# Fewer early weight pieces in the last chunk of an attention and two-MoE kernel, more in the two before it

## The chip, the cores and the metric

The kernel runs on one core of a Trainium2 chip. The metric is device time in microseconds (us) of one execution; three runs before the change took 767.27, 767.58 and 767.68 us.

## What is computed

Three parts, each feeding the next; the two layers' inner nonlinearities are softplus and silu.

```python
def _attn_ref(x, state):                     # x (4, 8, 512, 64), state (4, 8, 32, 64)
    scores = scale * np.matmul(x, state.transpose(0, 1, 3, 2))
    ...                                      # softmax over the 32 states
    xread = np.matmul(a, state)
    scores2 = scale * np.matmul(state, x.transpose(0, 1, 3, 2))
    ...                                      # softmax over the 512 tokens
    sread = np.matmul(a2, x)
    return np.concatenate([xread, sread], axis=2)

def _moe_ref(x, w_in, w_out):                # 2176 x 512, d_ff 2048
    h = x @ w_in
    g = np.maximum(h, 0.0) + np.log1p(np.exp(-np.abs(h)))
    return g @ w_out

def _moe2_ref(x, w_gate, w_val, w_out):      # d_ff 1536
    g = x @ w_gate
    silu = g * (1.0 / (1.0 + np.exp(-g)))
    val = x @ w_val
    return silu * val @ w_out
```

Weights arrive as 64-bit floats, seen by the kernel as pairs of 32-bit words.

## The kernel before

Every 32-bit matmul operand is split into a high and a low part (line 91: `low` is the subtraction of the high part), and a product is three matmuls (`mm3`, line 86). The first layer has four chunks of 512 hidden columns; in each chunk four batches of four tiles are worked through. One such tile is a step (a unit in the code), so chunk c is steps 16c to 16c+15, 64 in all. In step n TensorE does `p2` of step n (12 matmuls into the four banks py, at line 89 as all `mm3`), then what is hooked under "pe", then `p1` of step n+4 (6 matmuls into a bank ph). ScalarE takes two softplus copies from ph (h and C), GpSimd subtracts them (l), and p2 uses h and l. After the last tile of a batch VectorE adds the four py banks into yacc (`y_add`, line 453). A bank that these additions have not emptied can't be written again. The framework picks the banks of PSUM and the buffers of SBUF; in the built program step 20's first py group takes the bank of step 19's first addition and its second group that of the third, before and after the change. In step 60, before, only the fourth group takes a bank of step 59's additions; after, the third and the fourth do.

Weights are converted in pieces of 128 x 512. A piece is loaded raw (line 123), copied by ScalarE (`size`, line 132), put together by VectorE with one operation over the exponent words (`head`, line 136) and two with two operands (`tail`, lines 143 and 146), then split by ScalarE and GpSimd (`high`, `low`). A piece of the second layer (tag "made") is written back to DRAM for later use (lines 181, 199, 209). Two kinds: a gv piece (gate and value columns) also needs four GpSimd sums (line 193) and a second split, six GpSimd operations in all; a w piece (second output weight) needs one. The second layer has 36 pieces, three for each of 12 column groups: gv_0, gv_1, w. In names, gv5_1 is group 5's second gv piece and w25 is group 5's w piece (the printed names may leave numbers out, so a trace shows t_gv and t_w).

The first layer's loop (line 796) writes the order of ScalarE, VectorE, GpSimd and SP by hand: hooks by step and kind, run in the order load, pe, dve0, additions of dt 0 and 1, act, pool, additions of dt 2 and 3, dve1, act1. `at_weights` (line 721) hooks a piece with number n and lateness: load at n-4, size at n-1, head in dve0 of n, tail in dve1 of n+late, high and low at n+late+1. `EARLY` (lines 763 and 764) lists the steps of the second-layer pieces that are made inside the first layer, in the order gv0_0, gv0_1, w20, gv1_0, and so on. The remaining pieces are made in the second layer's loop, two steps of which take three pieces (line 835). In the last chunk VectorE also splits yacc (B11, B21) and forms the sums T1 to T4 (lines 469 to 475) that the second layer multiplies (px, pz, py). The second layer's weights come back from DRAM with `load_gw` (line 230).

Of the kernel before, what the change touches and what calls it, by code (L numbers as in the profile page):

```python
# [37 lines left out]
def attention_moe_moe2_kernel(  # L38
# [20 lines left out]
    NCK = F1 // CH  # L59
# [591 lines left out]
    with tc.manual_schedule(engines={ENG.PE}):  # L651
        units = [(c, b, ft) for c in range(NCK) for b in range(B) for ft in range(FT)]
        NU = len(units)
        UC = B * FT
# [66 lines left out]
        def at_weights(n, late, store, key, make):  # L721

            def begin():
                store[key] = make(*key)
            at(max(0, n - 4), "load", begin)
            for m, kind, step in (
                (n - 1, "act1", "size"), (n, "dve0", "head"), (n + late, "dve1", "tail"),
                (n + late + 1, "act", "high"), (n + late + 1, "pool", "low"),
            )[:3 if store is win else 5]:
                if m == FIRST - 1 and n == FIRST:  # L730
                    m, kind = FIRST, "load"
                if m >= FIRST:
                    at(m, kind, lambda step=step: getattr(store[key], step)())

        for c in range(NCK):
# [5 lines left out]
            for i, (store, make, key) in enumerate(pieces):  # L741
                n, late = n0 + i // 2 * FT + i % 2, 2 - 2 * (i % 2)
# [17 lines left out]
        ):  # L760
            at(i, kind, fn, 0)

        EARLY = [(c * UC + n, 0) for c in range(NCK - 1) for n in ((2, 6, 10, 14) if c else (11, 14, 15))]
        EARLY += [((NCK - 1) * UC + n, 0 if n % 4 else 2) for n in (0, 1, 2, 4, 5, 6, 8)]
        for j, (n, late) in enumerate(EARLY):
            at_weights(n, late, made, (j,), second_piece)
            at(n + late + 1, "pool", lambda j=j: made[j,].sums())
# [66 lines left out]

        for k, j in enumerate(range(len(EARLY), 3 * NF)):
            n, half = divmod(k, 2)
# [35 lines left out]
        with tc.manual_schedule(engines={ENG.DVE, ENG.SP}):  # L872
            run2(-1, "load0")
            run2(-1, "load1")
            for n in range(NS2):
                run2(n, "load0")
                run2(n, "load1")
                c = {}
# [86 lines left out]
```

## Time and profile before

| | us |
|---|---|
| median of 3 runs | 767.58 |
| profiled execution | 768.64 |
| its span, first to last instruction | 766.9 |
| TensorE busy (PE) | 732.2 |
| VectorE busy (DVE) | 439.3 |
| GpSimd busy (POOL) | 386.2 |
| ScalarE busy (ACT) | 318.9 |

The profile has one line for an instruction or a group of equal ones: start, duration, engine, source line, operation, output and inputs, count. A bracket at the end gives the idle time of that engine just before and what ended it. Starts are us from the span's start. The span is 1.7 us shorter than the execution. The granted clock is the share of TensorE's full speed that it was given. Step 16 begins at 142.15 us, step 32 near 219, step 48 near 296, and the second layer at 369.63.

### The profile page before, as it was taken

To read this page: it belongs to the slowest core of one execution; us is meant where nothing else is said; L and a number is where in the kernel's file an instruction comes from. 1 tells how busy PE (TensorE), PEld (TensorE's weight loads), DVE (VectorE), ACT (ScalarE), POOL (GpSimd) and SP (SyncE) were. 2 spreads that over 40 slices of the span, in tenths; PEclk is the share of its full clock that TensorE was granted. 3 is DMA by queue.
4 is the path that set the end of the run, shared out by engine and by line. 5 is a ranking of instruction groups with operands and counts; after the bars stand their busy time and mean duration, and the time that the engine had idled before them with its cause. 6 is when DMAs were issued, how large, how long until landed. Compare 5 with 4: busy or idle time off the path is not lost.

```text
span 766.9 us, 9998 instructions
## 1 busy us (share of the span) xinstructions
PE 732.2 (95%) x3640; PEld 571.1 (74%) x3640; DVE 439.3 (57%) x605; ACT 318.9 (42%) x584; POOL 386.2 (50%) x352
## 2 busy tenths in 40 slices
PE   2898999999999999997999999999999999999997
PEld 0455767777777777775778878788888888888885
DVE  4975627876577547589657555465453333343343
ACT  2774436544454445445454434343353223223320
POOL 1655626755565366787486665565462223223222
PEclk9589999999999999999999999999999999999999
DMA  9921103363344324557488998876646645436502
GB/s 349 409 80 56 60 24 107 119 214 138 106 119 160 110 97 151 194 218 221 163 298 309 300 359 302 312 278 235 203 146 236 219 156 224 170 116 221 211 2 109
DMA packets 51072, 143.78 MB, mean 187 GB/s; under 512 B 5712, under 2 KB 18000, under 8 KB 51024
## 3 DMA queue, kind: packets, MB, share of 16 engines
q1 hardware_dynamic: 51024, 143.15, 53.4%
q8 instruction: 28, 0.46, 0.2%
q14 instruction: 20, 0.16, 0.1%
HBM read 107.22 MB, written 35.91 MB: 187 GB/s over the span
## 4 chain that ended last, share of the span: by engine, by line
PE 81%; DMA 5%; DVE 5%; POOL 4%; ACT 2%; issue 2%; SPq 0%; ACTq 0%; DVEq 0%; POOLq 0%
PE py L89 22%; PE px L89 16%; PE po L89 16%; PE ph L89 9%; PE pz L89 7%; PE pt L89 3%; PE pm L374 2%; DMA gw<-gv_d 2%; DMA raw_gv<-in_moe_w_val_dram 2%; PE ps L505 2%; POOL l L92 1%; PE ps L89 1%; PE sc L267 1%; DMA xT<-in_xt_dram 1%; PE pa L335 1%
## 5 line engine op out<-in xcount | busy, mean ns | idle before, releaser
L89 PE MATMUL py<-h,wo 128*128 128x512 f32 x512 | 159.7, 393 | 8.7 <-DVE yacc L453 6.8
L92 POOL TENSOR_TENSOR l<-C,h 128x512 fp32r<-128x512 f32 x64 | 91.7, 1435 | 108.2 <-PE py L89 64.3
L89 PE MATMUL po<-w,h 128*128 128x512 f32 x384 | 126.2, 391 | 0.0
L89 PEld LDWEIGHTS py<-h,wo 128*128 128x128 f32 x512 | 96.2, 189 | 31.1 <-DVE yacc L453 7.6
L92 POOL TENSOR_TENSOR l<-cA,h 128x512 fp32r<-128x512 f32 x24 | 33.7, 1402 | 147.0 <-ACT h L574 147.0
L89 PE MATMUL ph<-aT,m 128*128 128x512 f32 x384 | 102.2, 401 | 0.5 <-POOL aT L92 0.5
L89 PE MATMUL py<-l,wo 128*128 128x512 f32 x256 | 100.0, 391 | 0.0
L89 PEld LDWEIGHTS ph<-aT,m 128*128 128x128 f32 x384 | 70.2, 188 | 28.9 <-issue 12.0
L595 DVE TENSOR_TENSOR oacc<-po,oacc 128x512 f32<-128x512 f32 x80 | 55.1, 690 | 60.5 <-PE po L89 60.0
L89 PEld LDWEIGHTS po<-w,h 128*128 128x128 f32 x384 | 72.1, 188 | 14.9
L404 ACT ACTIVATE h<-ph 128x512 fp32r<-128x512 f32 x64 | 38.2, 598 | 99.2 <-PE ph L89 61.6
L89 PE MATMUL po<-w,l 128*128 128x512 f32 x192 | 74.8, 390 | 0.5 <-POOL l L92 0.5
L89 PE MATMUL px<-T_0s,gw 128*128 128x512 f32 x216 | 61.5, 393 | 4.2 <-ACT cA L883 2.5
L89 PE MATMUL px<-T_1s,gw 128*128 128x512 f32 x216 | 60.7, 389 | 0.0
L89 PEld LDWEIGHTS py<-l,wo 128*128 128x128 f32 x256 | 48.3, 189 | 10.3
L89 PEld LDWEIGHTS px<-T_0s,gw 128*128 128x128 f32 x216 | 39.9, 188 | 14.6 <-ACT cA L883 3.6
L891 DVE TENSOR_TENSOR cA<-py,cA 128x512 f32<-128x512 f32 x24 | 16.6, 690 | 57.5 <-PE py L89 50.4
L574 ACT ACTIVATE h<-cA 128x512 fp32r<-128x512 f32 x24 | 15.1, 631 | 76.9 <-DVE cA L910 76.9
L89 PEld LDWEIGHTS px<-T_1s,gw 128*128 128x128 f32 x216 | 40.5, 188 | 8.5
L89 PEld LDWEIGHTS po<-w,l 128*128 128x128 f32 x192 | 36.0, 188 | 8.3 <-POOL l L92 1.0
L902 ACT ACTIVATE cC<-px 128x512 f32<-128x512 f32 x24 | 14.3, 597 | 64.2 <-PE px L89 60.8
L453 DVE TENSOR_TENSOR yacc<-py,yacc 128x512 f32<-128x512 f32 x48 | 31.5, 686 | 16.1 <-PE py L89 15.9
(147 smaller groups left out, 1348.4 us busy)
## 6 DMA issues: line engine op xcount, KB each, us to landing
gw<-gv_d SPq DMA_DIRECT2D x96, 512.0 KB, 6.5
gv_d<-gv SPq DMA_DIRECT2D x24, 512.0 KB, 3.2
gv_d<-split_gv SPq DMA_DIRECT2D x24, 512.0 KB, 3.5
w<-w_d SPq DMA_DIRECT2D x24, 512.0 KB, 9.2
raw_win<-in_moe_w_in_dram SPq DMA_DIRECT2D x16, 512.0 KB, 6.6
raw_wo<-in_moe_w_out_dram SPq DMA_DIRECT2D x16, 512.0 KB, 4.7
raw_gv<-in_moe_w_gate_dram SPq DMA_DIRECT2D x48, 128.0 KB, 4.4
raw_gv<-in_moe_w_val_dram SPq DMA_DIRECT2D x48, 128.0 KB, 4.1
```

Of the source, the lines that this page charges most:

```text
L89: nc.tensor.matmul(o, a[s], b[t], start=first and i == 0, stop=last and i == 2, **k)
L92: eng.tensor_tensor(out=o, in0=whole, in1=high.bitcast(F32), op=ALU.subtract)
L267: nc.tensor.matmul(self.sc[k * NS:(k + 1) * NS, :], st[q, k, b, :], xT[b, k // 2][q, k % 2, :], start=True, stop=True,)
L335: nc.tensor.transpose(self.ps[:, r * P:(r + 1) * P], self.e[:, r * P:(r + 1) * P], ident)
L374: nc.tensor.matmul(ps[k * NS:(k + 1) * NS, :], st[q, k, b, :], win[c, k].t[q, :], start=True, stop=True)
L404: nc.scalar.activation(self.h, self.ps, AF.Softplus)
L453: nc.vector.tensor_tensor(out=v, in0=yps[dt], in1=v, op=ALU.add)
L505: nc.tensor.matmul(ps, sw[:, kt, :], win[c, kt].t, start=kt == 0, stop=kt == KT - 1)
L574: nc.scalar.activation(h, src, AF.Copy)
L595: nc.vector.tensor_tensor(out=v, in0=ps, in1=v, op=ALU.add)
L891: nc.vector.tensor_tensor(out=c["A"], in0=y, in1=c["A"], op=ALU.add)
L902: nc.scalar.activation(c["C"], x, AF.Copy)
```

## The change

The list of steps at which the early pieces stand. Chunk 0 keeps three pieces; chunks 1 and 2 have six each where they had four (steps 2, 3, 6, 7, 10 and 14 of the chunk); the last chunk has three where it had seven (its steps 0, 1 and 2). The total of 18 stays.

```diff
-        EARLY = [(c * UC + n, 0) for c in range(NCK - 1) for n in ((2, 6, 10, 14) if c else (11, 14, 15))]
-        EARLY += [((NCK - 1) * UC + n, 0 if n % 4 else 2) for n in (0, 1, 2, 4, 5, 6, 8)]
+        EARLY = [(c * UC + n, 0) for c in range(NCK - 1) for n in ((2, 3, 6, 7, 10, 14) if c else (11, 14, 15))]
+        EARLY += [((NCK - 1) * UC + n, 0 if n % 4 else 2) for n in (0, 1, 2)]
```

VectorE around the additions of step 19 (yacc0), before: win2 are first-layer pieces, m1_3 the subtractions that empty two more banks, and the last number of a name counts buffers.

```order
L143 SCALAR_TENSOR_TENSOR t_gv1_0_1464<-raw_gv1_0_1264,t_gv1_0_1464 128x512
L146 SCALAR_TENSOR_TENSOR t_gv1_0_1464<-raw_gv1_0_1264,t_gv1_0_1464 128x512
L453 TENSOR_TENSOR yacc0_0_825<-py1_0_0_1384,yacc0_0_825 128x512
L453 TENSOR_TENSOR yacc0_0_825<-py1_0_1_1385,yacc0_0_825 128x512
L453 TENSOR_TENSOR yacc0_1_827<-py1_0_2_1386,yacc0_1_827 128x512
L453 TENSOR_TENSOR yacc0_1_827<-py1_0_3_1387,yacc0_1_827 128x512
L92 TENSOR_TENSOR m1_3_0_1536<-pm1_3_0_1513,m1_3_0_1536 128x512
L92 TENSOR_TENSOR m1_3_1_1538<-pm1_3_1_1518,m1_3_1_1538 128x512
```

The same place after the change:

```order
L143 SCALAR_TENSOR_TENSOR t_gv1_0_1469<-raw_gv1_0_1264,t_gv1_0_1469 128x512
L146 SCALAR_TENSOR_TENSOR t_gv1_0_1469<-raw_gv1_0_1264,t_gv1_0_1469 128x512
L136 TENSOR_SCALAR t_gv1_1_1504<-t_gv1_1_1504 128x512
L453 TENSOR_TENSOR yacc0_0_825<-py1_0_0_1389,yacc0_0_825 128x512
L453 TENSOR_TENSOR yacc0_0_825<-py1_0_1_1390,yacc0_0_825 128x512
L453 TENSOR_TENSOR yacc0_1_827<-py1_0_2_1391,yacc0_1_827 128x512
L453 TENSOR_TENSOR yacc0_1_827<-py1_0_3_1392,yacc0_1_827 128x512
L143 SCALAR_TENSOR_TENSOR t_gv1_1_1504<-raw_gv1_1_1318,t_gv1_1_1504 128x512
L146 SCALAR_TENSOR_TENSOR t_gv1_1_1504<-raw_gv1_1_1318,t_gv1_1_1504 128x512
L92 TENSOR_TENSOR m1_3_0_1548<-pm1_3_0_1524,m1_3_0_1548 128x512
L92 TENSOR_TENSOR m1_3_1_1550<-pm1_3_1_1529,m1_3_1_1550 128x512
```

A head has come ahead of the additions, and two tails between them and the m subtractions. Chunk 2 has the same at step 35.

VectorE ahead of the additions of step 55 (yacc1), before: B11 and B21 are splits of yacc.

```order
L136 TENSOR_SCALAR t_gv5_0_2986<-t_gv5_0_2986 128x512
L92 TENSOR_TENSOR B11_0_0s_2982<-yacc0_0_825,B11_0_0s_2982 128x512
L143 SCALAR_TENSOR_TENSOR t_gv5_0_2986<-raw_gv5_0_2789,t_gv5_0_2986 128x512
L146 SCALAR_TENSOR_TENSOR t_gv5_0_2986<-raw_gv5_0_2789,t_gv5_0_2986 128x512
L136 TENSOR_SCALAR t_gv5_1_3020<-t_gv5_1_3020 128x512
L92 TENSOR_TENSOR B11_0_1s_3014<-yacc0_0_825,B11_0_1s_3014 128x512
L143 SCALAR_TENSOR_TENSOR t_w24_2930<-raw_w24_2741,t_w24_2930 128x512
L146 SCALAR_TENSOR_TENSOR t_w24_2930<-raw_w24_2741,t_w24_2930 128x512
L143 SCALAR_TENSOR_TENSOR t_gv5_1_3020<-raw_gv5_1_2826,t_gv5_1_3020 128x512
L146 SCALAR_TENSOR_TENSOR t_gv5_1_3020<-raw_gv5_1_2826,t_gv5_1_3020 128x512
L92 TENSOR_TENSOR B21_0_0s_3049<-yacc0_1_827,B21_0_0s_3049 128x512
L453 TENSOR_TENSOR yacc1_0_980<-py3_1_0_2935,yacc1_0_980 128x512
```

The same place after:

```order
L92 TENSOR_TENSOR m3_3_1_2964<-pm3_3_1_2944,m3_3_1_2964 128x512
L537 TENSOR_TENSOR ys_1356<-ps33_3003,ys_1356 128x512
L92 TENSOR_TENSOR B11_0_0s_3033<-yacc0_0_825,B11_0_0s_3033 128x512
L92 TENSOR_TENSOR B11_0_1s_3062<-yacc0_0_825,B11_0_1s_3062 128x512
L92 TENSOR_TENSOR B21_0_0s_3090<-yacc0_1_827,B21_0_0s_3090 128x512
L453 TENSOR_TENSOR yacc1_0_980<-py3_1_0_2987,yacc1_0_980 128x512
```

Two heads and six tails have left this place.

VectorE ahead of the additions of step 59 (yacc2), before, its last ten rows:

```order
L136 TENSOR_SCALAR t_gv6_0_3415<-t_gv6_0_3415 128x512
L475 TENSOR_TENSOR T4_0_0_3185<-yacc0_1_827,T2_0_0_3179 128x512
L92 TENSOR_TENSOR T1_0_0s_3181<-yacc1_0_980,T1_0_0s_3181 128x512
L469 TENSOR_TENSOR T3_0_1_3211<-yacc1_1_983,yacc1_0_980 128x512
L143 SCALAR_TENSOR_TENSOR t_w25_3113<-raw_w25_2932,t_w25_3113 128x512
L146 SCALAR_TENSOR_TENSOR t_w25_3113<-raw_w25_2932,t_w25_3113 128x512
L471 TENSOR_TENSOR yacc1_0_980<-yacc1_0_980,yacc0_0_825 128x512
L92 TENSOR_TENSOR T3_0_0s_3213<-T3_0_0_3144,T3_0_0s_3213 128x512
L473 TENSOR_TENSOR T2_0_1_3255<-T3_0_1_3211,yacc0_0_825 128x512
L453 TENSOR_TENSOR yacc2_0_1140<-py3_2_0_3115,yacc2_0_1140 128x512
```

And after:

```order
L475 TENSOR_TENSOR T4_0_0_3191<-yacc0_1_827,T2_0_0_3185 128x512
L92 TENSOR_TENSOR T1_0_0s_3187<-yacc1_0_980,T1_0_0s_3187 128x512
L469 TENSOR_TENSOR T3_0_1_3217<-yacc1_1_983,yacc1_0_980 128x512
L471 TENSOR_TENSOR yacc1_0_980<-yacc1_0_980,yacc0_0_825 128x512
L92 TENSOR_TENSOR T3_0_0s_3219<-T3_0_0_3154,T3_0_0s_3219 128x512
L473 TENSOR_TENSOR T2_0_1_3259<-T3_0_1_3217,yacc0_0_825 128x512
L453 TENSOR_TENSOR yacc2_0_1140<-py3_2_0_3126,yacc2_0_1140 128x512
```

w25's two tails are gone (they stand in step 50 now), and the head of gv6_0, a piece of the second layer's loop, has moved ahead, to step 52.

## Rows read from the trace of the kernel before

**Rows 1.** The page's totals: busy us, share of the span, instructions of each engine.
```profile
PE 732.2 (95%) x3640; PEld 571.1 (74%) x3640; DVE 439.3 (57%) x605; ACT 318.9 (42%) x584; POOL 386.2 (50%) x352
```

**Rows 2.** Busy by stage: length, then PE, PEld, DVE, ACT, POOL; clock, DMA, GB/s.
```profile
157.70:175.00 17.30, 17.30 (x89) 13.64 (x89) 11.38 (x17) 7.08 (x13) 9.71 (x10) 1.00 0.49 168
...
311.00:334.00 23.00, 23.00 (x114) 18.10 (x113) 14.07 (x16) 11.63 (x22) 18.71 (x21) 1.00 0.58 206
334.00:354.00 20.00, 18.09 (x79) 14.29 (x77) 17.58 (x19) 10.85 (x22) 18.44 (x15) 1.00 0.70 244
354.00:369.60 15.60, 10.72 (x43) 8.89 (x44) 14.77 (x16) 5.20 (x10) 8.48 (x6) 0.89 0.74 257
369.60:500.00 130.40, 126.25 (x597) 104.45 (x596) 75.02 (x113) 57.16 (x100) 79.91 (x86) 1.00 0.81 290
```

**Rows 3.** TensorE in order of time, steps 55 to 60 and the second layer's start.
```profile
331.88 1.52 PE L89 MATMUL ph<-aT,m 128*128 128x512 f32 x6
...
336.35 0.73 PE L89 MATMUL py<-h,wo 128*128 128x512 f32 x2 [1.59 <-DVE yacc L453]
...
352.83 0.62 PE L89 MATMUL py<-h,wo 128*128 128x512 f32 x2
...
358.88 1.22 PE L89 MATMUL py<-h,wo 128*128 128x512 f32 x2 [5.20 <-DVE yacc L453]
...
369.63 0.84 PE L89 MATMUL px<-B_0s,gw 128*128 128x512 f32 x3
```

**Rows 4.** Busy by stage, the 3 us behind the longer wait.
```profile
358.88:361.92 3.04, 3.04 (x10) 2.51 (x11) 2.33 (x4) 0.51 (x2) 0.00 (x0) 0.52 1.10 256
```

**Rows 5.** VectorE in order of time, ahead of step 55's additions, first and last.
```profile
323.79 0.55 DVE L136 TENSOR_SCALAR t_gv<-t_gv 128x512 int32<-128x512 int32 x1 [3.26 <-ACT t_gv L132]
...
335.62 2.47 DVE L453 TENSOR_TENSOR yacc<-py,yacc 128x512 f32<-128x512 f32 x4
```

**Rows 6.** VectorE in order of time, ahead of step 59's additions.
```profile
340.79 0.94 DVE L92 TENSOR_TENSOR B_1s<-yacc,B_1s 128x512 fp32r<-128x512 f32 x1
...
349.71 1.78 DVE L143 SCALAR_TENSOR_TENSOR t_w<-raw_w,t_w 128x512 int32<-128x512 int32 x1
351.53 1.66 DVE L146 SCALAR_TENSOR_TENSOR t_w<-raw_w,t_w 128x512 int32<-128x512 int32 x1
...
358.14 2.47 DVE L453 TENSOR_TENSOR yacc<-py,yacc 128x512 f32<-128x512 f32 x4
```

**Rows 7.** VectorE in order of time, chunk 1, steps 18 to 23.
```profile
152.75 1.51 DVE L136 TENSOR_SCALAR t_gv<-t_gv 128x512 int32<-128x512 int32 x1
...
157.93 2.48 DVE L453 TENSOR_TENSOR yacc<-py,yacc 128x512 f32<-128x512 f32 x4
160.32 1.28 DVE L92 TENSOR_TENSOR m<-pm,m 128x512 fp32r<-128x512 f32 x2
...
170.07 0.69 DVE L146 SCALAR_TENSOR_TENSOR t_win<-raw_win,t_win 128x512 int32<-128x512 int32 x1
170.68 1.78 DVE L143 SCALAR_TENSOR_TENSOR t_gv<-raw_gv,t_gv 128x512 int32<-128x512 int32 x1
...
176.08 2.73 DVE L453 TENSOR_TENSOR yacc<-py,yacc 128x512 f32<-128x512 f32 x4 [2.89 <-PE py L89]
```

**Rows 8.** TensorE in order of time, step 20's py and the ph behind it.
```profile
160.22 0.62 PE L89 MATMUL py<-h,wo 128*128 128x512 f32 x2
...
165.68 1.52 PE L89 MATMUL ph<-aT,m 128*128 128x512 f32 x6
```

**Rows 9.** GpSimd in order of time, beside the tails of rows 7.
```profile
170.07 1.84 POOL L92 TENSOR_TENSOR l<-C,h 128x512 fp32r<-128x512 f32 x1 [3.00 <-PE py L89]
```

**Rows 10.** VectorE in order of time, chunk 2, the additions of step 39.
```profile
253.06 2.73 DVE L453 TENSOR_TENSOR yacc<-py,yacc 128x512 f32<-128x512 f32 x4 [2.91 <-PE py L89]
```

**Rows 11.** TensorE in order of time, the second layer's longest wait.
```profile
487.09 0.96 PE L89 MATMUL px<-T_0s,gw 128*128 128x512 f32 x3 [1.52 <-ACT cA L883]
```

**Rows 12.** DMA issues: count, KB each, median us to landing.
```profile
raw_win<-in_moe_w_in_dram SPq DMA_DIRECT2D x16, 512.0 KB, 6.6
```

## The prediction

> **What bounds the kernel now.** I read the totals first, then busy time by stage, then TensorE's instructions in order of time, then the queue of the engine it waits for. The totals: TensorE has matmuls in flight 95% of the span, so time comes back only where TensorE stands still or runs slowly [rows 1]. By stage, 311 to 334 us has no TensorE gap; 334 to 354 is short by 1.9 us of 20; 354 to 369.6 has 10.7 us of work in 15.6, at a granted clock of 0.89. That is the second half of the first layer's last chunk, steps 56 to 63. In the 130 us behind it, the start of the second layer, TensorE misses 4.2 us [rows 2]. What the reader is to see in the order of time: two idle times in brackets, 1.59 us inside step 56 and 5.20 us inside step 60, both ended by the VectorE additions of line 453 that empty the y banks of PSUM [rows 3]. Behind the second, 3.04 us pass at a granted clock of 0.52, TensorE's lower level (1.2 of 2.4 GHz) [rows 4].
>
> Why are the additions late? VectorE executes in written order. Step 55's matmuls end by 331.88, when the next ph begins [rows 3], but its additions begin at 335.62: from 323.79 on VectorE has three B subtractions, two heads and six tails of the pieces w24, gv5_0 and gv5_1 to do first, without an idle time [rows 5]. Ahead of step 59's additions, from 340.79 to 358.14, it is again never idle: ten operations for the T sums and their splits, w25's two tails (1.78 and 1.66 us) and one head [rows 6].
>
> **The change part by part.** The number of early pieces stays 18, so the second layer still prepares the same 18 later; no arithmetic is added or taken, and TensorE's queue keeps its order. Four pieces leave the last chunk (steps 52, 53, 54, 56), two more stand in chunks 1 and 2 each (steps 19 and 23, 35 and 39), and the pieces between shift their kind. A piece moved takes with it its load and its write-back on SP, two or three ScalarE copies, VectorE's head and two tails, and one (w) or six (gv) GpSimd operations.
>
> *Taken out, steps 52 to 55.* Without the pieces only the three B subtractions stand ahead of step 55's additions. At the slow end of such operations, 1.78 us, they take 5.3 us after 323.79 and are done by 329.1; the third waits for a copy that ScalarE makes in its own step, which may hold it to some 331.5 (an estimate: the step's end less little). TensorE asks for the first freed bank at 334.76 (336.35 less 1.59). An addition takes 0.62 us (2.47 for four [rows 5]), so it is 2.6 us early: 1.59 us come back. What is late next there is nothing on TensorE's path.
>
> *Taken out, steps 56 to 59.* The stretch of 17.35 us loses w25's tails, 3.44 us: 13.9 us remain. The additions of step 55 end by 334.0 (331.5 and four of 0.62), so T's ten operations end at about 347.9. TensorE would want the first addition's bank in step 60's third group, at 352.83 less the 1.59 gone before it, 351.2 [rows 3]: the addition must start by 350.6, and there are 2.7 us to spare. If all ten operations took 1.78 us (17.8), they would end at 351.8 and 1.2 us of the wait would stay; with all at 0.69 none. I take none, since the 13.9 us is this very stretch. So 5.20 us come back, and with the long wait goes the slow clock behind it: 3.04 us at 0.52 do the work of 1.58, so 1.46 us. The gains are 1.59 + 5.20 + 1.46 = 8.25 us.
>
> *Put in, chunk 1.* This is where it could cost. In step 19 the new head (gv1_1) stands ahead of the additions, its tails behind them and ahead of the two m subtractions. Before, the additions begin at 157.93, 0.62 us apart [rows 7]; TensorE's next py begins at 160.22 [rows 8] and wants the first bank then and the third 0.68 later: the third was 1.1 us early, the tightest. A head takes 0.55 [rows 5] to 1.51 us [rows 7]: a stall between 0 and 0.4. The two tails take 1.4 us (0.69 each) to 3.6 (1.78 each); with the head they push the m subtractions, which ended at 161.60 [rows 7], to between 163.5 and 166.7, while the matmuls that need their bank come at 165.68 [rows 8]: between 0 and 1.0 us. I take 0.4 us for both together, nearer the short form, since GpSimd is idle in part of that stretch. In step 23 the new head has an idle time of 2.89 us ahead of the additions to fall into, and in chunk 2 step 39's has 2.91 [rows 7, 10]; I take nothing. If that cover is gone, each us of lateness beyond it is one us of TensorE.
>
> One thing decides how long these tails take. At 170.07 a tail takes 0.69 us, and the next, beside GpSimd's subtraction l, takes 1.78, while l takes 1.84 [rows 7, 9]; the additions, with one operand in PSUM, keep 0.62 us apart. The Trainium skill says why (SBUF — State Buffer, "Who interferes with whom"): a VectorE operation with two SBUF inputs and a GpSimd operation that reads SBUF exclude each other for a whole instruction. The rows agree. The rule speaks against this change, since the pieces put in bring such operations on both engines at once; by it the tails there take the long form, the upper ends above, and the sum would be 6.85 us of gain in place of 7.85.
>
> *Queues.* On SP the loads of the new pieces go out four steps ahead, and a later load waits behind each write-back, which waits for GpSimd. A 512 KB weight load lands in a median of 6.6 us [rows 12], and four steps of 4.08 us are 16, so I cost them at nothing; a load 10 us late would show as ScalarE waiting for it. On ScalarE a copy waits for GpSimd's sums; the softplus behind it has three steps (12 us) of lead.
>
> *The sum.* 8.25 - 0.4 = 7.85 us. Against the profiled execution, 768.64 us (span 766.9), that is 760.8 (span 759.05). The median of the runs, 767.58, lies 1.06 us below that execution, so the forecast is 767.58 - 7.85 = 759.7 us.
>
> **The rivals.**
>
> A. T's chain stays late: step 59's additions still end behind TensorE. For it: ten operations beside GpSimd's l and B22 in 16 us; 1.2 us by the slow end, and as much again if the chain starts late for ScalarE's copies. Against: the 2.7 us of room. Time: 759.7 + 2.4 = about 762.1.
>
> B. The wait moves to the front: VectorE and GpSimd get behind in steps 18 to 24 as they did in steps 52 to 60, and the additions stall TensorE once in chunk 1 and once in chunk 2. For it: only 1.1 us to spare in chunk 1, and steps 52 to 55 before look the same, pieces in neighbouring steps. Against: from 157.7 to 175 VectorE is busy 11.4 of 17.3 us [rows 2]. Its price is that of the old stall, 5.20 + 1.46, twice, 13.3 us: 767.58 - 8.25 + 13.3 = 772.6. It decides from 4.1 us of stall per chunk on. The skill's exclusion rule would bring it about if the new tails and GpSimd operations all fell ahead of the additions; the order puts the tails behind them.
>
> C. The second layer gives it back: its start is held by transfers, not by TensorE. For it: TensorE waits up to 1.52 us there for ScalarE [rows 11], which waits for loads. Against: its loads are released by matmuls and by VectorE, so they move ahead with the layer. Time: all back, 767.6; half, 763.7.
>
> **How the numbers follow.** Forecast 0.70; A 0.12; C 0.12 (0.07 all, 0.05 half); B 0.06. A measurement of this kernel tells about 0.2%, 1.5 us, from no change. Faster: 0.70 + 0.12 + 0.05 = 0.87; same 0.07; slower 0.06. The range starts at 758.0: the forecast without the 0.4, and 1.3 us for one of the second layer's waits that may go. It ends at 763.7, with A and half of C inside; all of C and B, 0.13, stay out.
>
> **What would show it.** Right: in the last chunk no wait of py for the additions of line 453 over 0.3 us, no granted clock under 1.00 between the chunk's start and the second layer's first px, and that px near 361.8 us (369.63 [rows 3] less 7.85). The additions of step 19 begin 0.5 to 1.5 us later, and TensorE loses under 1 us around them. Wrong: TensorE waits for yacc or for m in steps 20 to 25 or 36 to 41 over 1 us; a wait stays in step 60; or px comes early and the end does not.

## The result, and the profile after

The changed kernel takes 758.12 us, median of four runs (757.59 to 758.71), against 767.42 for four of the kernel before (766.04 to 767.68): ratio 0.9877, interval 0.9858 to 0.9895, a gain of 9.4 us (8.1 to 10.9). Two later comparisons gave 0.9875 (0.9853 to 0.9898) and 0.9898 (0.9876 to 0.9920). Over all 16 runs of the one and 67 of the other the means are 758.67 and 767.39: 8.7 us, give or take 0.7. The forecast was 7.85. So the direction and the place were right and the size a little small; the first comparison alone (0.9877 of 767.42, 757.98) puts the time just under the lower end of my range, 758.0, while the difference of the means (767.58 less 8.72, 758.9) lies inside it.

The totals of the kernel after, one line as in [rows 1]:

```profile
PE 727.5 (96%) x3640; PEld 568.8 (75%) x3640; DVE 435.1 (57%) x605; ACT 320.1 (42%) x584; POOL 386.9 (51%) x352
```

By stage (length, then busy time of PE, PEld, DVE, ACT, POOL, granted clock, DMA share, GB/s), the stretches that answer to [rows 2]; the second layer now begins at 360.42:

```profile
156.00:177.00 21.00, 21.00 (x105) 16.45 (x104) 16.41 (x19) 10.37 (x19) 16.46 (x16) 1.00 0.63 217
310.00:333.00 23.00, 23.00 (x114) 18.10 (x113) 10.65 (x14) 11.26 (x21) 15.65 (x18) 1.00 0.61 213
333.00:351.00 18.00, 18.00 (x81) 14.92 (x80) 12.56 (x15) 7.45 (x14) 9.62 (x7) 1.00 0.41 165
351.00:360.40 9.40, 9.40 (x45) 7.79 (x44) 7.34 (x7) 3.65 (x7) 4.82 (x3) 1.00 0.01 2
360.40:490.00 129.60, 126.17 (x598) 104.58 (x597) 72.68 (x113) 57.20 (x100) 80.08 (x86) 1.00 0.81 292
```

The last chunk has no TensorE gap and no slow clock any more. TensorE after, in order of time: one new wait in step 24 of chunk 1, then the two places of [rows 3] without a bracket, and the second layer's first px.

```profile
180.02 0.73 PE L89 MATMUL py<-h,wo 128*128 128x512 f32 x2 [0.51 <-DVE yacc L453]
...
334.11 0.62 PE L89 MATMUL py<-h,wo 128*128 128x512 f32 x2
...
351.11 0.62 PE L89 MATMUL py<-h,wo 128*128 128x512 f32 x2
...
360.42 0.84 PE L89 MATMUL px<-B_0s,gw 128*128 128x512 f32 x3
```

VectorE after, the additions of steps 55 and 59 [rows 5, 6]: the first wait for TensorE now; of the second, the first addition (0.62 us) is done by 346.7, and TensorE wants a bank of theirs at 350.43, 3.7 us later.

```profile
329.55 2.73 DVE L453 TENSOR_TENSOR yacc<-py,yacc 128x512 f32<-128x512 f32 x4 [2.37 <-PE py L89]
...
346.08 2.52 DVE L453 TENSOR_TENSOR yacc<-py,yacc 128x512 f32<-128x512 f32 x4
```

Where the time went is read best by following the same TensorE instruction through two traces: TensorE's order is equal, so the difference of the two start times, taken at fixed places, says what each stretch won or lost. Against the kernel before, in us (worked out so from the traces; times in the head are of the kernel before):

| | before 66 | chunk 0, to 152 | chunk 1, to 219 | chunk 2, to 285 | to 334 | to 352 | to 369 | layer 2, to 500 | span |
|---|---|---|---|---|---|---|---|---|---|
| after | -1.58 | +0.29 | +0.80 | 0 | 0 | -1.91 | -6.81 | -0.84 | -10.04 |
| after, again (e1) | +0.36 | +0.28 | +0.87 | 0 | 0 | -1.91 | -6.81 | -0.85 | -8.04 |
| after, third (e12) | -1.90 | +0.20 | +0.83 | 0 | 0 | -1.91 | -6.81 | -0.88 | -10.47 |
| before, again (e5) | -2.72 | -0.05 | 0 | 0 | 0 | -0.03 | +0.83 | -1.39 | -3.36 |
| 3, 4, 5, 6 (e2) | -1.91 | -0.51 | 0 | 0 | 0 | -0.13 | -2.34 | -1.07 | -5.97 |
| sums later (e3) | -1.55 | +0.29 | 0 | 0 | 0 | -1.91 | -6.81 | -0.35 | -10.36 |
| pairs (e4) | -2.35 | +0.30 | 0 | +0.91 | +1.26 | -1.91 | -6.81 | -0.01 | -8.63 |
| 3, 5, 6, 4 (e6) | -1.84 | +0.01 | +0.39 | 0 | 0 | -1.91 | -6.81 | -0.09 | -10.26 |
| 3, 7, 7, 3 (e7) | -1.50 | +0.23 | 0 | +1.15 | +0.48 | -1.91 | -6.81 | +0.47 | -7.88 |
| e3, raw loads first (e8) | -2.29 | +0.21 | 0 | 0 | 0 | -1.91 | -6.81 | +4.00 | -6.79 |
| the same from step 5 (e9) | -2.98 | +0.31 | 0 | 0 | 0 | -1.91 | -6.81 | -2.33 | -13.72 |
| 3, 4, 6, 5 (e10) | -1.59 | +0.03 | 0 | 0 | 0 | -1.91 | -5.46 | +1.25 | -7.69 |
| e3, four buffers (e11) | -1.49 | +0.23 | 0 | 0 | 0 | -1.91 | -6.81 | -0.32 | -10.32 |

The first column has nothing to do with the change (e1, e5). Behind it the change wins 8.46, 8.40 and 8.57 us; against the second trace of the kernel before (e5) the same three win 7.8, 7.8 and 7.9.

### The profile page after: what moved, and what is told of

It reads as the page before. It is cut to its first block, busy times and chain, and to the rows that moved or that the text cites. A ratio compares the mean times of both kernels' runs of the same rounds, so it can differ in the third digit from the quotient of the medians.

```text
span 756.8 us, 9969 instructions
## 1 busy us (share of the span) xinstructions
PE 727.5 (96%) x3640; PEld 568.8 (75%) x3640; DVE 435.1 (57%) x605; ACT 320.1 (42%) x584; POOL 386.9 (51%) x352
## 4 chain that ended last, share of the span: by engine, by line
PE 79%; DMA 9%; POOL 4%; DVE 3%; ACT 2%; issue 1%; SPq 1%; POOLq 0%; ACTq 0%; DVEq 0%
PE py L89 23%; PE px L89 16%; PE po L89 15%; PE ph L89 10%; PE pz L89 7%; DMA raw_gv<-in_moe_w_val_dram 3%; PE pt L89 3%; DMA raw_win<-in_moe_w_in_dram 2%; PE ps L505 2%; PE pm L374 2%; DMA xT<-in_xt_dram 1%; DMA xn<-in_xn_dram 1%; POOL l L92 1%; PE ps L89 1%; POOL sums_gv L193 1%
## 5 line engine op out<-in xcount | busy, mean ns | idle before, releaser
L92 POOL TENSOR_TENSOR l<-cC,h 128x512 fp32r<-128x512 f32 x24 | 31.9, 1329 | 16.1 <-ACT h L574 14.7
```

The costliest lines, as they stand in the source:

```text
L92: eng.tensor_tensor(out=o, in0=whole, in1=high.bitcast(F32), op=ALU.subtract)
```

## The experiments

**e1 and e12, the changed kernel again; e5, the kernel before again.** No edit.

> The changed kernel again, for the size of its gain. The two profiled executions differ by 10.0 us of span: 8.5 us in the first layer's last chunk, 0.9 in the second layer, 0.95 lost in chunk 1, and 1.57 us that are won before step 0, where nothing was changed. Theory 1: the 1.57 us are chance of one execution (the half-clock stretch at the start was 27.3 us before and 17.1 us after); then the gain over several pairs is 8.4 us, ratio 0.989. Theory 2: they come with the change; then the gain is 10.0 us, ratio 0.987, and every start of this kernel shows the short stretch.

> The kernel before, run as if it were a new one, for what a comparison of runs says where nothing is changed. In the traces so far the changed kernel gains 8.5 us behind step 0 in both of its profiled executions, and its start lies at -1.58 and at +0.36 us against the kernel before; its runs give 9.5 us. Theory 1: the surplus of about 1 us is the start's chance, which also shifts this comparison: its ratio differs from 1 by up to 0.002, and its profiled execution differs from the earlier one by more than 0.5 us before step 0 and by less than 0.3 us behind it. Theory 2: the start is part of what the change does: ratio 1.000 within 0.0005 and the start within 0.3 us of the earlier trace.

> The changed kernel a third time, against the kernel before on one chip. Theory 1: the gain is what the traces give behind step 0, 8.4 us, plus up to 0.8 where the slow clock behind step 60's wait lasts twice as long in the kernel before: a mean difference of 8.4 to 9.2 us. Theory 2: something that the traces don't show adds to it: a mean difference over 9.6 us. Chunk 1 loses 0.7 to 0.9 us at step 24 again and chunk 3 gains 8.7.

Measured: e1 758.1 us and e12 759.28 (ratios above; e12's means differ by 7.8); e5 766.81, ratio 0.9994 (0.9978 to 1.001). The start is chance: two traces of the changed kernel lie 1.94 us apart before step 0, two of the kernel before 2.72. What differs there is, among other things, the granted clock, here by stage over the first 46 us, of before, after and e1:

```profile
0.00:46.00 46.00, 29.35 (x339) 13.24 (x339) 33.35 (x68) 24.12 (x52) 18.73 (x22) 0.70 0.90 349
```

```profile
0.00:46.00 46.00, 27.56 (x348) 12.77 (x352) 33.93 (x72) 25.62 (x56) 19.27 (x23) 0.81 0.90 349
```

```profile
0.00:46.00 46.00, 28.98 (x339) 13.11 (x339) 32.96 (x67) 23.75 (x51) 18.46 (x22) 0.70 0.90 349
```

It is not the clock alone: e5 has 0.81 like the changed kernel and starts 1.14 us ahead of it, and e7 has 1.00 and starts no earlier. So theory 1 of e1 holds, although its run time (ratio 0.9875) fitted theory 2 better: the trace separates what the runs can't. e5 contradicts one part of its theory 1: behind step 0 the same program differed by more than 0.3 us. Its trace, TensorE's waits in order of time, and the 6.85 us behind the second one by stage:

```profile
333.58 0.73 PE L89 MATMUL py<-h,wo 128*128 128x512 f32 x2 [1.59 <-DVE yacc L453]
356.10 1.22 PE L89 MATMUL py<-h,wo 128*128 128x512 f32 x2 [5.23 <-DVE yacc L453]
...
483.73 0.96 PE L89 MATMUL px<-T_0s,gw 128*128 128x512 f32 x3 [0.63 <-ACT cA L883]
```

```profile
356.15:363.00 6.85, 6.85 (x23) 5.55 (x24) 6.02 (x8) 3.65 (x7) 2.71 (x2) 0.67 0.98 316
```

The two waits are the same to 0.03 us, but the slow clock behind the second one lost 0.83 us more than in [rows 4], and a wait of 1.52 us in the second layer [rows 11] was 0.63. The kernel before pays its long wait with a slow stretch of changing length, so the gain in chunk 3 is 8.7 us against the one execution and 9.5 against the other. e12's difference (7.8) is below the 8.4 to 9.2 of its theory 1, by less than its interval (6.1 to 9.5 us), and rules out theory 2.

**e2 and e6: which of the pieces taken from chunk 3 made the waits.** Both against the changed kernel's lists.

```diff
changed kernel:
-        EARLY = [... for n in ((2, 3, 6, 7, 10, 14) if c else (11, 14, 15))]
-        EARLY += [... for n in (0, 1, 2)]
e2:
+        EARLY = [... for n in ((11, 14, 15), (2, 6, 10, 14), (2, 3, 6, 10, 14))[c]]
+        EARLY += [... for n in (0, 1, 2, 4, 5, 6)]
e6:
+        EARLY = [... for n in ((11, 14, 15), (2, 3, 6, 10, 14), (2, 3, 6, 7, 10, 14))[c]]
+        EARLY += [... for n in (0, 1, 2, 8)]
```

> Pieces 3, 4, 5, 6: chunk 3 loses only step 56's piece (w25); steps 52 to 54 still have three (gv5_0, gv5_1, w25). Theory 1 (each stall has its own cause): step 55's additions stay late and the stall of 1.6 us in step 56 stays within 0.6; ahead of step 59's additions 3.4 us of tails leave the stretch of 17.35 us, so the stall of 5.20 falls to about 1.6 and the slow clock behind it goes: 767.4 - 3.6 - 1.5 = 762.3. Theory 2 (one lateness that builds up from step 52 on): without relief in steps 52 to 54 the T sums start as late as before and wait for ScalarE, the stall in step 60 stays over 4 us, and the time is above 765.

> Pieces 3, 5, 6, 4: the counterpart of the run with 3, 4, 5, 6. Steps 52 to 54 lose their three pieces, step 56 keeps w25. Theory 1 (step 60's wait is the sum of a late start of the T sums and of w25's tails): step 55's additions are in time, no wait in step 56; the T operations start about 4 us earlier but keep 3.4 us of tails, so they end within 1 us of the need: a wait of 0 to 1.0 us in step 60, no fall of the clock, chunk 3 at -7.5 to -8.7 us against the kernel before. Theory 2 (w25's two tails alone make the wait): the wait in step 60 is still 3 us or more and chunk 3 gains under 5 us.

Measured: e2 763.12 us, ratio 0.9947 (0.9926 to 0.9967); e6 758.38, a single run. TensorE in e2:

```profile
332.63 0.73 PE L89 MATMUL py<-h,wo 128*128 128x512 f32 x2 [0.28 <-DVE yacc L453]
...
345.17 0.50 PE L89 MATMUL py<-l,wo 128*128 128x512 f32 x1 [0.92 <-POOL l L92]
...
353.10 1.22 PE L89 MATMUL py<-h,wo 128*128 128x512 f32 x2 [2.63 <-DVE yacc L453]
```

VectorE in e6, from step 55's additions to step 59's:

```profile
328.59 2.73 DVE L453 TENSOR_TENSOR yacc<-py,yacc 128x512 f32<-128x512 f32 x4 [2.22 <-PE py L89]
...
337.71 0.76 DVE L92 TENSOR_TENSOR T_0s<-yacc,T_0s 128x512 fp32r<-128x512 f32 x1 [0.94 <-ACT T_0s L485]
...
338.99 1.77 DVE L143 SCALAR_TENSOR_TENSOR t_w<-raw_w,t_w 128x512 int32<-128x512 int32 x1
340.80 0.69 DVE L146 SCALAR_TENSOR_TENSOR t_w<-raw_w,t_w 128x512 int32<-128x512 int32 x1
...
345.42 2.47 DVE L453 TENSOR_TENSOR yacc<-py,yacc 128x512 f32<-128x512 f32 x4
```

e6 carries w25's tails at the old place and has no wait in steps 56 to 60; its chunk 3 gains the whole 8.72 us, which is theory 1 at its best end (the 0.39 that it loses in chunk 1 falls at step 24, as in the changed kernel). e2 without them there still waits 2.63 us. So without the pieces of steps 52 to 54 w25's tails cost nothing, and with those pieces a wait stays even when the tails go; beside them the tails made the wait longer, 5.20 us against 2.63. In e6 VectorE has idle time ahead of the second half of T (0.94 us, against 4.13 in the changed kernel, waiting for ScalarE), so that the tails take time that was idle there.

How the pieces make T late in e2 is not VectorE's own work alone. The first half of T is done by 341.1, and then VectorE waits for ScalarE's copy of T, which stands behind a copy that waited for GpSimd's sums of a gv piece:

```profile
341.41 0.64 ACT L197 ACTIVATE split_gv<-sums_gv 128x512 fp32r<-128x512 f32 x1 [5.46 <-POOL sums_gv L193]
...
343.42 0.63 ACT L485 ACTIVATE T_0s<-yacc 128x512 fp32r<-128x512 f32 x1
```

```profile
344.09 1.58 DVE L92 TENSOR_TENSOR T_0s<-yacc,T_0s 128x512 fp32r<-128x512 f32 x1 [3.03 <-ACT T_0s L485]
```

This is read from the trace; no run separates it there. It is the wait for ScalarE of e2's theory 2, though the wait of TensorE is not the 4 us of that theory. e2's time bore out its theory 1 (762.3 expected), but its wait in step 56 fell to 0.28 where 1.0 to 2.2 was expected, its wait in step 60 is 2.63 where 1.6 was, and 0.92 for l came in step 59: the pieces were worth more at the one place and less at the other.

**e3 and e4: what the new wait in step 24 is.** The changed kernel in chunk 1, VectorE from the additions of step 19 to those of step 23:

```profile
156.82 2.48 DVE L453 TENSOR_TENSOR yacc<-py,yacc 128x512 f32<-128x512 f32 x4
159.21 0.68 DVE L143 SCALAR_TENSOR_TENSOR t_gv<-raw_gv,t_gv 128x512 int32<-128x512 int32 x1
159.93 1.66 DVE L146 SCALAR_TENSOR_TENSOR t_gv<-raw_gv,t_gv 128x512 int32<-128x512 int32 x1
161.51 1.27 DVE L92 TENSOR_TENSOR m<-pm,m 128x512 fp32r<-128x512 f32 x2
...
172.20 0.99 DVE L136 TENSOR_SCALAR t_w<-t_w 128x512 int32<-128x512 int32 x1 [3.02 <-ACT t_w L132]
173.12 1.78 DVE L143 SCALAR_TENSOR_TENSOR t_win<-raw_win,t_win 128x512 int32<-128x512 int32 x1
...
179.29 2.47 DVE L453 TENSOR_TENSOR yacc<-py,yacc 128x512 f32<-128x512 f32 x4
```

VectorE has time to spare ahead of its lateness: at 172.20 it has waited 3.02 us for ScalarE's copy of w21, and from there to the additions it is busy without a break. ScalarE, and the GpSimd sums that it waits for:

```profile
170.91 0.63 ACT L197 ACTIVATE split_gv<-sums_gv 128x512 fp32r<-128x512 f32 x1 [1.38 <-POOL sums_gv L193]
171.44 0.65 ACT L132 ACTIVATE t_w<-raw_w 128x512 f32<-128x512 f32 x1
```

```profile
159.23 1.80 POOL L92 TENSOR_TENSOR gv<-t_gv,gv 128x512 fp32r<-128x512 f32 x1 [0.48 <-ACT gv L152]
...
166.90 1.74 POOL L92 TENSOR_TENSOR gv<-t_gv,gv 128x512 fp32r<-128x512 f32 x1
...
170.41 0.46 POOL L193 TENSOR_TENSOR sums_gv<-t_gv,sums_gv 128x128 f32<-128x128 f32 x1
```

```diff
e3:
+            wait = 1 if n in (UC + 3, 2 * UC + 3) else 0
-            at(n + late + 1, "pool", lambda j=j: made[j,].sums())
-            at(n + late + 2, "act", lambda j=j: made[j,].split_sums())
+            at(n + late + 1 + wait, "pool", lambda j=j: made[j,].sums())
+            at(n + late + 2 + wait, "act", lambda j=j: made[j,].split_sums())
e4:
-for n in ((2, 3, 6, 7, 10, 14) if c else (11, 14, 15))]
+for n in ((11, 14, 15), (2, 6, 7, 10, 14, 15), (2, 6, 7, 10, 14, 15))[c]]
```

> The changed kernel with the GpSimd sums of the pieces of steps 19 and 35 one step later (in step 21 and 37, their second split in 22 and 38). Theory 1: the lateness of step 23's additions (3.2 us against the kernel before, and 0.51 us of idle TensorE in step 24) comes from ScalarE's queue: the copy split_gv waits to 170.91 for GpSimd's sums, and the copy of w21 behind it releases VectorE only at 172.2. With the sums later w21's copy goes out about 1.7 us earlier, the additions begin at least 1.5 us earlier and the idle time of 0.51 us goes: time 0.5 to 0.8 us below the changed kernel. Theory 2: VectorE has too many operations in the long form there; then the additions come no more than 0.5 us earlier, the stall stays between 0.3 and 0.8 us and the time is the same.

> The same numbers 3, 6, 6, 3, but in chunks 1 and 2 at the steps 2, 6, 7, 10, 14 and 15, so that the two neighbours are always a gv piece and a w piece, which has one GpSimd operation instead of six. Theory 1 (the cost of chunk 1 is the second gv piece's GpSimd sums ahead of a ScalarE copy): no idle time over 0.2 us for yacc or m in chunks 1 and 2, and 0.5 to 0.9 us less time than the changed kernel. Theory 2 (the cost is the number of pieces in the chunk): TensorE still loses 0.5 to 1 us in chunk 1, at another step, and the time is that of the changed kernel within 0.3 us.

Measured: e3 757.87 us, ratio 0.9875 (0.9853 to 0.9897); e4 759.89, ratio 0.9906 (0.9883 to 0.9928). VectorE in e3 at the same place:

```profile
170.20 1.01 DVE L136 TENSOR_SCALAR t_w<-t_w 128x512 int32<-128x512 int32 x1 [0.99 <-ACT t_w L132]
...
176.38 2.47 DVE L453 TENSOR_TENSOR yacc<-py,yacc 128x512 f32<-128x512 f32 x4
```

The copy goes 2.0 us earlier, step 23's additions 2.9 us (the tails behind the head are shorter too, 0.95 and 0.83 us in place of 1.78 and 1.66), and the 0.80 us of chunk 1 are gone in the trace: theory 1 of e3. In the run times its worth can't be told from nothing, and the second layer came out 0.49 worse, which is within what it moves by itself (e5). The same neighbours stand in chunk 2, and in the changed kernel VectorE waits for the same copy there:

```profile
249.30 1.00 DVE L136 TENSOR_SCALAR t_w<-t_w 128x512 int32<-128x512 int32 x1 [2.48 <-ACT t_w L132]
...
255.28 2.48 DVE L453 TENSOR_TENSOR yacc<-py,yacc 128x512 f32<-128x512 f32 x4
```

These additions of step 39 begin 0.5 us before TensorE's step 40, those of step 23 began 1.3 us after the start of step 24. So 1.8 us decide between the loss of 0.80 and none.

e4 has no such neighbours and no wait in chunk 1 either, but loses 2.2 us at two places that the changed kernel doesn't have, for m:

```profile
221.06 1.66 PE L89 MATMUL ph<-aT,m 128*128 128x512 f32 x6 [0.64 <-DVE m L92]
...
299.33 1.66 PE L89 MATMUL ph<-aT,m 128*128 128x512 f32 x6 [1.02 <-DVE m L92]
```

VectorE ahead of the second of these, step 47's additions, the tails of its w piece, then m:

```profile
292.83 2.47 DVE L453 TENSOR_TENSOR yacc<-py,yacc 128x512 f32<-128x512 f32 x4
295.23 1.75 DVE L143 SCALAR_TENSOR_TENSOR t_w<-raw_w,t_w 128x512 int32<-128x512 int32 x1
297.01 1.66 DVE L146 SCALAR_TENSOR_TENSOR t_w<-raw_w,t_w 128x512 int32<-128x512 int32 x1
298.59 1.27 DVE L92 TENSOR_TENSOR m<-pm,m 128x512 fp32r<-128x512 f32 x2
```

Neither theory of e4 said that. It is what the prediction feared at step 20: tails between the additions and the m subtractions, both in the long form, make m late. With the number unchanged, the place of the pieces decided where and how much they cost.

**e7 and e10: more pieces early, and fewer.**

```diff
e7 (with the later sums, at steps 19 and 39):
+        EARLY = [... for n in ((11, 14, 15), (2, 3, 6, 7, 10, 11, 14), (2, 3, 6, 7, 10, 11, 14))[c]]
e10:
+        EARLY = [... for n in ((11, 14, 15), (2, 6, 10, 14), (2, 3, 6, 7, 10, 14))[c]]
+        EARLY += [... for n in (0, 1, 2, 4, 8)]
```

> Twenty early pieces, 3, 7, 7, 3 (steps 2, 3, 6, 7, 10, 11 and 14 of chunks 1 and 2; the GpSimd sums of steps 19 and 39 one step later). Theory 1 (the second layer's waits follow from the pieces made in it): with 16 instead of 18 there, its px waits for ScalarE fall from 3.1 us to under 2, chunks 1 and 2 lose at most 1 us together, and the time is 0 to 1.5 us below the changed kernel. Theory 2 (chunks 1 and 2 are full with six): they lose 1.5 us or more to waits for m or yacc, and the time is above the changed kernel's.

> Pieces 3, 4, 6, 5: chunk 1 as before the change, chunk 2 as after it, and in the last chunk steps 48, 49, 50, 52 and 56, so that between step 50 and step 56 one piece is left of three. Theory 1 (VectorE's lateness in steps 52 to 54 is a sum, and one piece fits into the time to spare): no wait for yacc over 0.3 us in chunk 3, chunk 3 at -8.0 to -8.8 us against the kernel before, chunk 1 at 0: 757.0 to 758.0. Theory 2 (any gv piece there makes the additions late): a wait of 1 us or more in step 56 or 60, chunk 3 gains under 7 us, time above 759.

Measured: e7 760.43 us, ratio 0.9897 (0.9869 to 0.9926); e10 760.16, ratio 0.9901 (0.9879 to 0.9924). e7 loses 1.63 us in chunk 2 and at the start of chunk 3 (a wait of 0.87 for yacc at 218.90 among them), and the second layer is no faster with two pieces less: theory 2 in the loss. That the time is longer than the changed kernel's is not clear from six runs (757.28 to 761.51). e10's waits:

```profile
350.56 0.73 PE L89 MATMUL py<-h,wo 128*128 128x512 f32 x2 [1.05 <-DVE yacc L453]
...
477.80 0.96 PE L89 MATMUL px<-T_0s,gw 128*128 128x512 f32 x3 [1.79 <-ACT cA L883]
```

```profile
478.00:482.00 4.00, 4.00 (x12) 3.12 (x12) 0.47 (x1) 2.53 (x5) 3.48 (x5) 0.60 0.89 241
```

One gv piece in step 52 with w25 in step 56 costs 1.35 us of chunk 3, and the px wait of 1.79 in the second layer drew a granted clock of 0.60 behind it, where waits of 1.52 [rows 11] and 1.59 us drew none. The length of the wait does not settle it: in e7 a px wait of 2.08 us drew none (granted clock 1.00 from 476 to 490 us). Theory 1 was wrong by these 1.35 us. Theory 2 had the wait and the time, but not the reason: chunk 3 still gains 7.4, and the rest of the time went in the second layer (1.25 us, no more than it moves by itself, e5).

**e8, e9 and e11: the second layer's px waits.** In the changed kernel ScalarE's copy for a w piece waits 2.82 us for its raw load and holds up cA behind it. SP issued that load at 462.90, behind six reloads of 512 KB. Each step of that layer's loop makes two pieces (the line behind 835 is `n, half = divmod(k, 2)`), not three in two of its steps.

```profile
474.40 0.66 ACT L132 ACTIVATE t_w<-raw_w 128x512 f32<-128x512 f32 x1 [2.82 <-DMA raw_w<-in_moe_w_out_dram]
...
476.39 0.58 ACT L883 ACTIVATE cA<-px 128x512 f32<-128x512 f32 x1
```

```diff
all three, on top of e3:
-    RAWS = {"raw": 2, "raw0": 6}
+    RAWS = {"raw": 4, "raw0": 6}
e8 (e11 has none of what follows):
-            at2(n - 1, f"load{half}", begin)
+            at2(max(n - 2, -1), "end" if n >= 2 else f"load{half}", begin)
...
+                run2(n, "end")
                 if n + 2 < NS2:
                     load_gw(n + 2)
e9, in place of e8's at2:
+            at2(*((n - 2, "end") if n >= 5 else (n - 1, f"load{half}")), begin)
```

> The kernel with the sums of steps 19 and 35 one step later, four raw buffers instead of two, and in the second layer the raw loads issued ahead of the reloads of the weights. Theory 1 (the px waits of 0.4 to 1.5 us come from raw loads that are issued behind 3 MB of weight reloads: raw_w issued at 462.90 lands at 474.40): the waits px for cA go to under 0.4 us in total, and the time is 1.0 to 1.8 us below the changed kernel, 756.3 to 757.1. Theory 2 (DMA as a whole is the limit there): another transfer is late in its place, and the time is within 0.5 us of the changed kernel.

> As the run with four raw buffers, but the raw loads go ahead of the reloads only from the pieces of the second layer's step 5 on. In the run before, that order cost 2.96 us of idle TensorE in step 1 (ScalarE's copy for a piece of the next step, scheduled ahead of cC, waited for a raw load) and took away the later px waits of 0.36 and 0.88 us. Theory 1 (both effects are local): the second layer lies 0.8 to 1.3 us below the kernel with the sums one step later, no px wait over 0.4 us behind 430 us, time about 756.8. Theory 2 (the reloads of the weights then land late): pz or px wait 0.5 us or more for gw, and the time is at or above 757.9.

> The kernel with the sums one step later and four raw buffers, raw loads in the old order behind the reloads. Theory 1 (the order decides): the later px waits of about 0.4 and 0.9 us stay, the time is within 0.6 us of 757.9. Theory 2 (the buffers decide, since SP no longer waits for a raw buffer): they go as in the run with both edits, and the time is 756.6 or less.

Measured: e8 761.92 us, ratio 0.9928 (0.9905 to 0.9950); e9 756.14, ratio 0.9850 (0.9827 to 0.9873); e11 758.69, ratio 0.9891 (0.9870 to 0.9912). In e8 the late px waits went, but the new order made another:

```profile
381.36 0.66 ACT L132 ACTIVATE t_gv<-raw_gv 128x512 f32<-128x512 f32 x1 [2.15 <-DMA raw_gv<-in_moe_w_val_dram]
381.92 0.58 ACT L903 ACTIVATE cC<-px 128x512 f32<-128x512 f32 x1
```

A copy for the next step now stands ahead of cC on ScalarE and waits for its load; TensorE idles 2.96 us for cC there, and reloads of gw land late further on. Used from the layer's step 5 on (e9) the order keeps the one effect without the other: the only wait for cA left is 0.40 us, and the layer is 2.0 us shorter than in e3. e11 shows that the four buffers alone do not do it: px waits of 0.42 and 1.56 stay. The new order with two buffers was not run. e9 lies 2.3 us under the changed kernel, in the mean of the runs and behind step 0 in the trace (10.74 us won against 8.46).

## Why the prediction was right or wrong

*Steps 52 to 55.* Right in cause: step 55's additions wait for TensorE, and the wait of 1.59 us is gone. The stretch gained 1.91. A bracket understates a wait: start to start, 0.51 us of idle time cost 0.80 (chunk 1), 0.64 cost 0.91 and 1.02 cost 1.26 (e4). Without a wait the next matmul begins 0.16 us before the profile ends the last one (0.39 us long, 0.23 apart), and the first two behind a wait take 0.73 us in place of 0.62. I summed brackets.

*Steps 56 to 59.* 5.20 + 1.46 = 6.66 forecast, 6.81 measured. The reason was half wrong. I counted w25's two tails (3.44 us) out of the stretch; by e6 they may stay, and by e2 their going alone leaves 2.63 us of wait. That the pieces of steps 52 to 54 go does it. And the 1.46 of slow clock was one execution's: e5 shows 0.83 more.

*Chunk 1.* This is the step whose mechanism failed. I priced 0.4 us at step 20, for the tails ahead of the m subtractions, and nothing at step 23, because VectorE had 2.89 us of idle time there to spare. Step 20 lost nothing: the head took 0.42 us, so that step 19's additions began 0.2 us later against TensorE and not 0.5 to 1.5; the tails took 0.68 and 1.66 us, and m was done at 162.78, 1.6 us before the ph that needs it. Step 24 lost 0.80. I looked at the idle time of the engine that gets the work, and wrote of ScalarE's copy waiting for GpSimd's sums only that softplus behind it has lead; the next piece's copy stands behind it too, and that copy releases VectorE (e3). Chunk 0 lost 0.2 to 0.3 more at 128.65 us, without a bracket, in each kernel with six or seven pieces in chunk 1 and in e2 with four, but not in e6 and e10 with five and four; its cause stays open.

*Chunk 2 and the queues at nothing:* right in the time, 0 in all three traces of the changed kernel, but by 1.8 us of margin and not by the cover alone: in step 38 VectorE waits for ScalarE's copy as in step 22.

*The sum.* Forecast 8.25 - 0.4 = 7.85. In the traces behind step 0: 8.72 in chunk 3, less 0.80 and 0.29, plus 0.84 in the second layer, 8.47. Against e5's trace of the kernel before: 9.52 in chunk 3, less 0.80 and 0.34, less 0.55 in the second layer, 7.8. The second layer I left out; that it gains by the change is not shown, since the same program (e5) moved there by 1.39.

*The range* began too high, at 758.0. The mis-sized term is the gain of 8.25 us in chunk 3, which measured 8.72 against the one trace and 9.52 against the other: I took the brackets for the cost of the waits, and one execution's slow clock (1.46, in e5 2.29) for the cost of that. Chunk 1's miss of 0.4 us went the other way and hid part of it. Below the forecast the range allowed for the 0.4 and for one wait of the second layer, and for no longer slow stretch. I took 0.2% for what a measurement tells, but runs of the kernel before go from 764.48 to 771.74, and start, slow clock and second layer each move by 0.8 to 3 us between executions of one program. How much of the first comparison's 9.4 us is such scatter stays open; the mean over all runs, 8.7 give or take 0.7, agrees with the 7.8 to 8.6 of the traces.

*The rivals.* A: no; the T sums end in time, with 3.7 us to spare where 2.7 was worked out. B: a wait does come to chunk 1, with 0.80 us of the 4.1 that would decide. C: no; the second layer came out 0.84 us ahead of one trace of the kernel before and 0.55 behind the other, far from half the gain. The Trainium skill (SBUF — State Buffer, "Who interferes with whom") states that a VectorE instruction with two SBUF inputs contends with a GpSimd instruction that reads SBUF. The rows of chunk 1 agree: the tail at 159.21, begun 0.02 us ahead of GpSimd's subtraction, took 0.68 us, that subtraction 1.80 where the one before it took 1.29, and the tail at 159.93, begun while it ran, 1.66. The 6.85 us that I worked out by the rule supposed every tail in the long form, and one of two took it.

## What to carry to other kernels

When work is moved to a place with idle time, look up what ended that idle time: if it is another engine's in-order queue, ask what the moved work puts ahead of the releasing instruction there. Pieces of work upstream can look like too much work at the wait; test each by leaving it in its place and taking out the other (e2, e6). For effects under 1%, compare start times of the same instruction in two traces, and profile an unchanged kernel twice before believing a stretch.

## What the runs showed of the hardware

An idle TensorE cost 0.24 to 0.32 us more than the bracket shows, over five waits of 0.51 to 1.02 us. Waits of 1.79 (e10), 2.63 (e2), 2.96 (e8) and 5.2 us were followed by a lower granted clock, 0.50 to 0.60 over the next 3 to 4 us (its lower level is 1.2 of 2.4 GHz); waits of 1.52 and 1.59 were not, nor was one of 2.08 (e7), and the slow stretch behind the same 5.2 us was not equally long twice. The clock at the kernel's start changes from one execution to the next: from 0.70 to 1.00 over the first 46 us.
